# Half-array transposes, each half into its own PSUM bank, and all PSUM as one ring of four two-bank tiles

## The chip, the cores and the metric

The kernel runs on one core of a Trainium2 chip. The metric is the device time of one execution in microseconds. Engines are named as in the profile: PE (TensorE matmul), PEld (its weight loads), DVE (VectorE), ACT (ScalarE), POOL (GpSimd) and SP (SyncE, which issues the transfers).

## What is computed

Attention with a learned position bias, for 4 batches, 8 heads, 576 positions and head size 64, then a low-rank token mix and a channel MLP on the heads side by side (512 wide, hidden layer 2048):

```python
# attention: bias is a small MLP of the positions, for each head
scores = scale * np.matmul(q, k.transpose(0, 1, 3, 2))
h = np.maximum(x @ w1 + b1, 0.0)          # x[i, j] = log1p|i-j| / log1p(max(i, 1))
scores = scores + (h @ w2).transpose(2, 0, 1)[None]
attn = np.exp(scores - np.max(scores, axis=-1, keepdims=True))
attn = attn / (np.sum(attn, axis=-1, keepdims=True) + 1e-09)
o = np.matmul(attn, v)
# then, with x the heads side by side, (4, 576, 512)
u = x + (x.transpose(0, 2, 1) @ U @ V).transpose(0, 2, 1)
out = u + np.maximum(u @ w_ch1, 0.0) @ w_ch2
```

## The kernel before

The work goes in stages; the order on each engine is the order of the code (the schedule is manual).

**Bias** (0 to 68 us of the profiled execution). Tiles `bs` of the position MLP, written to DRAM and read back as `bias`. The first head pair is started among them.

**Attention** (68 to 396 us). Two heads are a pair; 16 pairs, each in nine slots, `slot(p, s)`. Slot 0 takes the last 64 rows of both heads, slots 1 to 8 one block of 128 query rows of one head. A slot's score product `sc` (L359) is made on PE by 64-row halves of the array: the two halves hold the same 64 numbers of head size against two halves of the keys, and write two banks of one tile. DVE adds the bias and takes the row minimum (L363), ACT takes the exponential (L382), and PE transposes the result, 128x128 blocks, by products with an identity: `tb` (L429, four blocks, in the slots 3 to 8 and in 0 and 1 of the pair behind), `tm` (L437), `ti` (L446, L449). DVE or ACT copies them to SBUF (L411 and L409 through `copy`). `av` (L465, tile `o`) multiplies with `v`: once for the first half of the query rows at the end of slot 8 (o0 from here on), once for the second half in slot 2 of the next pair (o1). `assemble` transposes its output back (`tx`, L483, L485). The slots carry other work besides: the conversion of the weights from 64-bit words (`conv_ops`: ACT L206, L209, DVE L212, L218, L224, POOL L229), the split of the next pair's operands into high and low parts on POOL (`hi` L178, `lo` L184), and from pair 4 on the token mix of the batch behind (`mt` L504, `mh` L523 to L525, in pairs 5, 9 and 13).

**MLP** (from 355 us, mixed with the end of attention until 396 us, alone after that). A round has two transposes of the input (`tu`, L581), `ph` (L608, 48 products), and `po` twice (L631, 24 products in all). `ph` is read by ACT (L613) and then DVE (L614), `po` by DVE (L634). In the rounds from 408 to 445 us DVE, ACT and POOL convert the next group's weights as well.

**PSUM** has eight banks. Before, `sc`, `bs` and `ph` come from two two-bank tiles (psS; a third, psX, while the bias stage lasts), `o` and every second `po` from one bank (psA), and all transposes, `mt`, `mh` and the other `po` from three single banks (psT and psT2).

The lines that decide which buffer a product waits for, and a transpose with its copy:

```python
rot = {"s": [psS], "t": [psT, psT2, psT2]}                   # after the bias stage
bank = psum("t", [P, 4, P], "tb")
for kb in range(4):
    nc.tensor.transpose(bank[:, kb, :], src[:, b0 + kb * P : b0 + (kb + 1) * P], ident)
copy(eng, pt[:, 5 * hd : 5 * hd + 4, o : o + P], bank)
```

Of the kernel before, what the change touches and what calls it, by code (L numbers as in the profile page):

```python
# [8 lines left out]
F32 = mybir.dt.float32  # L9
# [6 lines left out]
PSUM = bass.MemoryType.PSUM  # L16
# [4 lines left out]
DM = H * D  # L21
# [4 lines left out]
P = 128  # L26
# [25 lines left out]
def kernel(  # L52
# [282 lines left out]
    def scores(p, s):  # L335
# [4 lines left out]
        ps = psum("s", [P, 2, 512], "sc")  # L340
# [80 lines left out]

    def tr(p, c, hd, eng):
        hf, o = q_off(c)
        pt = get_pt(p, hf)
        src = pair[p]["P"][c]
        bank = psum("t", [P, 4, P], "tb")
        b0 = 0 if hd == 0 else S + LEFT
        for kb in range(4):
            nc.tensor.transpose(bank[:, kb, :], src[:, b0 + kb * P : b0 + (kb + 1) * P], ident)  # L429
        copy(eng, pt[:, 5 * hd : 5 * hd + 4, o : o + P], bank)  # L430

    def tr_m(p, eng):
        pt = get_pt(p, 0)
        pm = pair[p]["pm"]
        bank = psum("t", [P, 4, P], "tm")
        for kb in range(4):
            nc.tensor.transpose(bank[:, kb, :], pm[:, kb * P : (kb + 1) * P], ident)  # L437
        for hd in range(2):
            copy(eng, pt[:, 5 * hd : 5 * hd + 4, 0:LEFT], bank[:, :, hd * LEFT : (hd + 1) * LEFT])

    def tr_mid(p, hf, eng):
        pt = get_pt(p, hf)
        d = pair[p]
        bank = psum("t", [P, 4, P], "ti")
        for i in range(2):
            nc.tensor.transpose(bank[:, i, :], d["P"][2 * hf + i][:, 4 * P : 5 * P], ident)  # L446
        o = LEFT if hf == 0 else 0
        if hf == 0:
            nc.tensor.transpose(bank[:, 2, :], d["pm"][:, 4 * P : 5 * P], ident)  # L449
        copy(eng, pt[:, 4, o : o + 2 * P], bank[:, 0:2, :].rearrange("p a b -> p (a b)"))  # L450
        if hf == 0:
            copy(eng, pt[0:LEFT, 4, 0:LEFT], bank[0:LEFT, 2, 0:LEFT])
            copy(eng, pt[LEFT:P, 4, 0:LEFT], bank[LEFT:P, 2, LEFT:P])

    def av(p, hf):
        d = pair[p]
# [15 lines left out]
        ot = otp.tile([P, 320], F32, tag="ot", name="ot")
        copy("a", ot[:, 0:n], o[:, 0:n])
        d["ot", hf] = ot

    def assemble(p, hf):
# [3 lines left out]
        bank = psum("t", [P, 4, P], "tx")  # L480
        o = LEFT if hf == 0 else 0
        for i in range(2):
            nc.tensor.transpose(bank[:, i, :], ot[:, o + i * P : o + (i + 1) * P], ident)  # L483
        if hf == 0:
            nc.tensor.transpose(bank[0:LEFT, 2, :], ot[:, 0:LEFT], ident)  # L485
# [4 lines left out]
            in0=bank[:, 0:2, :].rearrange("p c (h d) -> p c h d", h=2),  # L490
# [3 lines left out]
        if hf == 0:  # L494
            copy("d", x_sb[0:LEFT, 4, hp * P : (hp + 1) * P], bank[0:LEFT, 2, :])
# [3 lines left out]
    def mix_t(b):  # L499
        t = psum("t", [P, DM], "mt")  # L500
# [77 lines left out]
    def make_ut(j, i):  # L578
        bank = psum("t", [P, KD, P], "tu")
# [16 lines left out]
    def mlp1(n):  # L596
# [23 lines left out]
    def mlp2(n):  # L620
# [3 lines left out]
        def step(i):  # L624
            ps = psA.tile([P, DM], F32, tag="a", name="po") if i % 2 else psum("t", [P, DM], "po")
# [340 lines left out]
```

## Time and profile before

| | us |
|---|---|
| median of 3 runs | 778.06 (776.85 to 778.28) |
| the profiled execution's own time | 778.02 |
| its span, first to last instruction | 776.0 |

| engine | busy us | share of the span |
|---|---|---|
| PE | 751.6 | 97% |
| DVE | 437.2 | 56% |
| ACT | 355.2 | 46% |
| POOL | 204.2 | 26% |

The share of busy time is a mean over stages with different limits, and a busy PE is not a PE at its peak: a matmul counts as busy while it is under way, and several are under way at once. Which wait ends last in a stage is read from timelines: one row is a run of like instructions on an engine, with its start, its duration, and in brackets the idle time ahead of it and what ended that.

### The profile page before, as it was taken

To read this page: it belongs to the slowest core of one execution; us is meant where nothing else is said; L and a number is where in the kernel's file an instruction comes from. 1 tells how busy PE (TensorE), PEld (TensorE's weight loads), DVE (VectorE), ACT (ScalarE), POOL (GpSimd) and SP (SyncE) were. 2 spreads that over 40 slices of the span, in tenths; PEclk is the share of its full clock that TensorE was granted. 3 is DMA by queue.
4 is the path that set the end of the run, shared out by engine and by line. 5 is a ranking of instruction groups with operands and counts; after the bars stand their busy time and mean duration, and the time that the engine had idled before them with its cause. 6 is when DMAs were issued, how large, how long until landed. Compare 5 with 4: busy or idle time off the path is not lost.

```text
span 776.0 us, 14159 instructions
## 1 busy us (share of the span) xinstructions
PE 751.6 (97%) x5452; PEld 593.7 (77%) x5452; DVE 437.2 (56%) x953; ACT 355.2 (46%) x827; POOL 204.2 (26%) x222
## 2 busy tenths in 40 slices
PE   6888999999999999999999999999999999999998
PEld 4325777666656675777889899889999999999886
DVE  7994577688877885663348844762147722221222
ACT  6995777677667775774115522441114410110010
POOL 0012545444444443630005601550005500000000
PEclk9999999999999999999999999999999999999999
DMA  5898953443344334540053300230003200001111
GB/s 182 277 312 267 292 158 93 134 133 107 106 140 133 109 94 116 160 166 2 21 191 97 109 13 28 89 102 1 1 14 96 69 1 1 1 28 55 55 41 68
DMA packets 46514, 78.77 MB, mean 102 GB/s; under 512 B 7920, under 2 KB 14576, under 8 KB 46448
## 3 DMA queue, kind: packets, MB, share of 16 engines
q1 hardware_dynamic: 46208, 77.62, 32.7%
q8 instruction: 43, 0.70, 0.4%
q10 hardware_dynamic: 240, 0.26, 0.1%
q14 instruction: 23, 0.19, 0.1%
HBM read 55.43 MB, written 22.43 MB: 100 GB/s over the span
## 4 chain that ended last, share of the span: by engine, by line
PE 78%; ACT 8%; DVE 8%; DMA 3%; issue 2%; POOL 1%; SPq 1%; ACTq 0%; DVEq 0%; POOLq 0%
PE po L631 24%; PE ph L608 23%; PE o L465 8%; PE sc L359 8%; PE tb L429 6%; PE bs L287 3%; DVE wt L218 2%; ACT p L382 2%; ACT pt L409 1%; DVE p L363 1%; PE tm L437 1%; PE mt L504 1%; DVE wt L212 1%; PE tx L483 1%; ACT ring L275 1%
## 5 line engine op out<-in xcount | busy, mean ns | idle before, releaser
L613 ACT ACTIVATE hh<-ph 128x1024 fp32r<-128x1024 f32 x36 | 36.9, 1026 | 207.2 <-PE ph L608 207.2
L614 DVE SCALAR_TENSOR_TENSOR hh<-ph,hh 128x1024 fp32r<-128x1024 f32 x36 | 44.1, 1225 | 140.2 <-ACT hh L613 140.2
L229 POOL TENSOR_TENSOR wy<-wt,wy 128x256 int32<-128x256 int32 (+1 forms) x68 | 50.0, 735 | 272.9 <-DVE wt L224 244.7
L382 ACT ACTIVATE p<-p,st 128x576 f32<-128x576 f32 x128 | 99.9, 781 | 38.1 <-DVE st L363 38.1
L363 DVE CUSTOM_DVE_ANT_0 p<-sc,bias 128x576 f32<-128x576 f32 x128 | 96.2, 751 | 25.8 <-PE sc L359 16.8
L631 PE MATMUL po<-wq,hh 128*128 128x512 f32 x432 | 103.2, 394 | 0.0
L631 PE MATMUL po<-w2q,hh 128*128 128x512 f32 x432 | 101.7, 390 | 0.4 <-DVE acc L634 0.4
L608 PE MATMUL ph<-ut,w1q 128*128 128x256 f32 x768 | 94.0, 280 | 0.0
L608 PEld LDWEIGHTS ph<-ut,w1q 128*128 128x128 f32 x768 | 91.9, 188 | 2.1 <-issue 1.2
L631 PEld LDWEIGHTS po<-wq,hh 128*128 128x128 f32 x432 | 80.1, 188 | 17.5
L631 PEld LDWEIGHTS po<-w2q,hh 128*128 128x128 f32 x432 | 79.9, 188 | 16.7 <-issue 0.6
L608 PEld LDWEIGHTS ph<-ut,wq 128*128 128x128 f32 x768 | 90.0, 188 | 1.4
L634 DVE TENSOR_TENSOR acc<-po,acc 128x512 f32<-128x512 f32 x72 | 49.6, 689 | 73.1 <-PE po L631 73.1
L608 PE MATMUL ph<-ut,wq 128*128 128x256 f32 x768 | 90.2, 277 | 0.0
L465 PE MATMUL o<-pt,v 128*64 128x320 f32 (+1 forms) x640 | 88.7, 411 | 0.6 <-ACT pt L409 0.6
L429 PE MATMUL tb<-ident,p 128*128 128x128 f32 x512 | 82.2, 283 | 3.4 <-DVE x_sb L411 1.8
L465 PEld LDWEIGHTS o<-pt,v 128*64 128x64 f32 x640 | 50.8, 136 | 27.6 <-issue 3.0
L429 PEld LDWEIGHTS tb<-ident,p 128*128 128x128 f32 x512 | 55.0, 140 | 20.9 <-issue 11.7
L409 ACT COPY pt<-tb 128x512 f32<-128x512 f32 x88 | 50.9, 579 | 30.4 <-PE tb L429 30.2
L359 PE MATMUL sc<-hi 64*128 64x288 f32 (+1 forms) x320 | 62.4, 386 | 1.9 <-DVE st L363 1.8
L184 POOL TENSOR_TENSOR lo<-raw,hi 128x896 fp32r<-128x896 f32 x30 | 63.2, 2108 | 2.2
L359 PEld LDWEIGHTS sc<-hi 64*128 64x128 f32 (+1 forms) x320 | 29.0, 178 | 40.0 <-issue 32.1
(94 smaller groups left out, 1024.6 us busy)
## 6 DMA issues: line engine op xcount, KB each, us to landing
wraw<-in_w_ch_dram SPq DMA_DIRECT2D x64, 256.0 KB, 2.7
raw<-in_qk_dram SPq DMA_DIRECT2D x32, 288.0 KB, 4.6
bias_dram<-ring SPq DMA_DIRECT2D x26, 295.5 KB, 3.3
v<-in_vp_dram SPq DMA_DIRECT2D x16, 320.0 KB, 3.6
bias<-bias_dram SPq DMA_DIRECT2D x16, 288.0 KB, 4.4
acc<-u_dram SPq DMA_DIRECT2D x18, 256.0 KB, 4.9
out_dram<-acc SPq DMA_DIRECT2D x18, 256.0 KB, 2.0
bias<-bias_dram SPq DMA_DIRECT2D x16, 256.0 KB, 4.9
```

The source lines that it names most:

```text
L184: eng.tensor_tensor(out=lo[:, a:e], in0=raw[:, a:e], in1=hi[:, a:e].bitcast(F32), op=ALU.subtract)
L229: nc.gpsimd.tensor_tensor(out=st["y"], in0=st["t"], in1=st["y"], op=ALU.add)
L359: mm(ps[0:n, a, 0:HALF], lhsT=q[r, q0 : q0 + n], rhs=k[r, k0 : k0 + HALF], start=(i == 0), stop=(i == len(terms) - 1),)
L363: nc.vector.tensor_tensor_reduce(out=halves(dst), in0=ps[:, :, 0:HALF], in1=halves(bias[hp][:, s * S : (s + 1) * S]), scale=-0.125, scalar ...
L382: nc.scalar.activation(out=dst, in_=dst, func=AF.Exp, bias=st[:, s : s + 1], scale=-1.0, accum_out=st[:, 10 + s : 11 + s])
L409: nc.scalar.copy(out=out, in_=in_)
L429: nc.tensor.transpose(bank[:, kb, :], src[:, b0 + kb * P : b0 + (kb + 1) * P], ident)
L465: mm(o[hd * D : (hd + 1) * D, 0:n], lhsT=v[:, vb * D : (vb + 1) * D], rhs=pt[:, pb, :], start=(j == 0), stop=(j == 4),)
L608: mm(st["ps"][:, f, :], lhsT=w, rhs=u[:, k, :], start=(i == 0), stop=(i == 3 * KD - 1))
L614: nc.vector.scalar_tensor_tensor(out=hl[n], in0=st["ps"], scalar=0.0, in1=hh[n].bitcast(F32), op0=ALU.max, op1=ALU.subtract)
L631: mm(ps, lhsT=h, rhs=w, start=(m == 0), stop=(m == 3 * FG - 1))
L634: nc.vector.tensor_tensor(out=a, in0=ps, in1=a, op=ALU.add)
```

## The change

Every transpose of attention is made by two products of half the rows. The source's rows 0 to 63 go through the upper half of the array into one bank, rows 64 to 127 through the lower half into the next bank. The copies read both banks at once and put the halves side by side; they move as many elements as before. The transposes `tu` of the MLP stay whole. And PSUM becomes one ring: each tile of the program, whatever it holds, takes two banks, and the buffer of the fourth tile before it.

```diff
-    psS = ctx.enter_context(tc.tile_pool(name="psS", bufs=2, space=PSUM))
-    psT = ctx.enter_context(tc.tile_pool(name="psT", bufs=1, space=PSUM))
-    psA = ctx.enter_context(tc.tile_pool(name="psA", bufs=1, space=PSUM))
...
-    def psum(tag, shape, name):
-        rot[tag].append(rot[tag].pop(0))
-        return rot[tag][-1].tile(shape, F32, tag=tag, name=name)
+    ps4 = ctx.enter_context(tc.tile_pool(name="ps4", bufs=4, space=PSUM))
+
+    def psum(name):
+        return ps4.tile([P, 2, 512], F32, tag="ps", name=name)
...
+    def flip(bank, i, src, a):
+
+        for h in range(2):
+            r = slice(h * D, (h + 1) * D)
+            nc.tensor.transpose(bank[:, h, i * D : (i + 1) * D], src[r, a : a + P], ident[r, r])
+
     def tr(p, c, hd, eng):
...
-        bank = psum("t", [P, 4, P], "tb")
+        bank = psum("tb")
         b0 = 0 if hd == 0 else S + LEFT
         for kb in range(4):
-            nc.tensor.transpose(bank[:, kb, :], src[:, b0 + kb * P : b0 + (kb + 1) * P], ident)
-        copy(eng, pt[:, 5 * hd : 5 * hd + 4, o : o + P], bank)
+            flip(bank, kb, pair[p]["P"][c], b0 + kb * P)
+        copy(
+            eng,
+            pt[:, 5 * hd : 5 * hd + 4, o : o + P].rearrange("p k (h q) -> p h k q", h=2),
+            bank[:, :, 0 : 4 * D].rearrange("p h (k q) -> p h k q", k=4),
+        )
...
-        o = psA.tile([P, 512], F32, tag="a", name="o")
+        o = psum("o")[:, 0, :]
...
-        bank = psum("t", [P, KD, P], "tu")
+        bank = psum("tu")[:, 0, :].rearrange("p (k q) -> p k q", k=KD)
...
-                st["ps"] = psum("s", [P, FG, TB], "ph")
+                st["ps"] = psum("ph").rearrange("p a (b t) -> p (a b) t", t=TB)
...
-            ps = psA.tile([P, DM], F32, tag="a", name="po") if i % 2 else psum("t", [P, DM], "po")
+            ps = psum("po")[:, 0, :]
```

`tm`, `ti` and `tx` are changed as `tb` is, `mt`, `mh`, `sc` and `bs` take their tile as `o` and `ph` do.

On PE, the end of a pair: slot 8's scores, the transposes of the last attention output (`tx`) and of slot 8 (`tb`), and the first product of o0. Before:

```order
L359 MATMUL sc<-hi 128x288 [waits DVE_49]
L359 MATMUL sc<-hi 128x288
L359 MATMUL sc<-lo,hi 128x288 x2
L359 MATMUL sc<-hi,lo 128x288 x2
L483 MATMUL tx<-ident,ot 128x128 [waits Activation_49]
L483 MATMUL tx<-ident,ot 128x128
L429 MATMUL tb<-ident,p 128x128 [waits DVE_49,PE_49,Activation_49]
L429 MATMUL tb<-ident,p 128x128 x3
L465 MATMUL o<-pt,v 64x320 [waits DMAHW7_49]
```

The same place after:

```order
L352 MATMUL sc<-hi 128x288 [waits Activation_49]
L352 MATMUL sc<-hi 128x288
L352 MATMUL sc<-lo,hi 128x288 x2
L352 MATMUL sc<-hi,lo 128x288 x2
L419 MATMUL tx<-ident,ot 128x64 [waits DVE_49,PE_49]
L419 MATMUL tx<-ident,ot 128x64 x3
L419 MATMUL tb<-ident,p 128x64 [waits DVE_49,Activation_49]
L419 MATMUL tb<-ident,p 128x64 x7
L471 MATMUL o<-pt,v 64x320 [waits DMAHW7_49,DVE_49]
```

Six whole transposes have become twelve halves, and o0, which waited for no other engine's work on PSUM, waits for DVE now: the fourth tile before it is the `tb` of slot 7, which DVE copies out. In pair 0 it is the score tile of slot 7.

On PE, one round of the MLP while weights are converted (`ut` is the transposed input, `w1q` and `w2q` the weights, `hh` the hidden layer). Before:

```order
L581 MATMUL tu<-ident,acc 128x128 [waits DMAHW1_49,DVE_49]
L581 MATMUL tu<-ident,acc 128x128 x3
L581 MATMUL tu<-ident,acc 128x128 [waits DMAHW2_49,DVE_49]
L581 MATMUL tu<-ident,acc 128x128 x3
L608 MATMUL ph<-ut,w1q 128x256 [waits Activation_49]
L608 MATMUL ph<-ut,w1q 128x256 x47
L631 MATMUL po<-w2q,hh 128x512 [waits DVE_49,Activation_49]
L631 MATMUL po<-w2q,hh 128x512 x11
```

After:

```order
L591 MATMUL tu<-ident,acc 128x128 [waits DMAHW5_49,DVE_49]
L591 MATMUL tu<-ident,acc 128x128 x3
L591 MATMUL tu<-ident,acc 128x128 [waits DMAHW6_49,DVE_49]
L591 MATMUL tu<-ident,acc 128x128 x3
L618 MATMUL ph<-ut,w1q 128x256 [waits DVE_49,Activation_49]
L618 MATMUL ph<-ut,w1q 128x256 x47
L641 MATMUL po<-w2q,hh 128x512 [waits DVE_49,Activation_49]
L641 MATMUL po<-w2q,hh 128x512 x11
```

The products are the same. `ph` waits for DVE besides: a round has five tiles, so the fourth tile before `ph` is the first `po` of the round behind, which DVE adds to the accumulator (L634). The second `tu` takes the buffer of the `ph` of the round behind.

## Rows read from the trace of the kernel before

**Rows 1.** Page, part 4: the chain that ended last, share of the span by engine and line

```profile
PE po L631 24%; PE ph L608 23%; PE o L465 8%; PE sc L359 8%; PE tb L429 6%; PE bs L287 3%; DVE wt L218 2%; ACT p L382 2%; ACT pt L409 1%; DVE p L363 1%; PE tm L437 1%; PE mt L504 1%; DVE wt L212 1%; PE tx L483 1%; ACT ring L275 1%
```

**Rows 2.** Busy us of each engine in a stretch, granted clock, DMA share, GB/s

```profile
core 0: us, PE busy (x) PEld busy (x) DVE busy (x) ACT busy (x) POOL busy (x), PEclk, DMA share, GB/s
42.20:45.50 3.30, 3.23 (x24) 0.81 (x24) 3.30 (x11) 3.30 (x9) 0.00 (x0) 0.50 0.94 302
80.00:356.00 276.00, 271.01 (x2194) 186.69 (x2193) 198.47 (x508) 194.51 (x486) 122.79 (x114) 1.00 0.47 135
```

**Rows 3.** Timeline of PE, pair 7: start, duration, engine, line, operation, count, idle before

```profile
181.22 0.29 PE L359 MATMUL sc<-lo,hi 64*64 64x288 f32 x2
181.36 0.29 PE L359 MATMUL sc<-hi,lo 64*64 64x288 f32 x2
...
182.76 0.66 PE L429 MATMUL tb<-ident,p 128*128 128x128 f32 x4
183.25 0.38 PE L446 MATMUL ti<-ident,p 128*128 128x128 f32 x2
...
195.89 2.91 PE L465 MATMUL o<-pt,v 128*64 128x320 f32 x20
```

**Rows 4.** Timeline of PEld, pair 7, slots 1 and 2

```profile
182.16 0.19 PEld L359 LDWEIGHTS sc<-hi 64*128 64x128 f32 x2 [0.17 <-issue]
...
182.76 0.42 PEld L429 LDWEIGHTS tb<-ident,p 128*128 128x128 f32 x4 [0.17 <-issue]
```

**Rows 5.** Timeline of DVE, pair 7

```profile
185.56 0.88 DVE L212 TENSOR_SCALAR wt<-wt 128x256 f32<-128x256 f32 x1 [0.52 <-ACT wt L206]
186.47 2.15 DVE L218 TENSOR_SCALAR wt<-wt 128x256 int32<-128x256 int32 x1
188.55 0.74 DVE L363 CUSTOM_DVE_ANT_0 p<-sc,bias 128x576 f32<-128x576 f32 x1
...
195.44 0.69 DVE L411 COPY pt<-tb 128x512 f32<-128x512 f32 x1
...
199.94 0.76 DVE L363 CUSTOM_DVE_ANT_0 praw<-sc,bias 128x576 f32<-128x576 f32 x1 [2.29 <-PE sc L359]
```

**Rows 6.** Timeline of ACT, pair 7

```profile
191.91 0.65 ACT L409 COPY pt<-tm 128x256 f32<-128x256 f32 x2 [0.44 <-PE tm L437]
```

**Rows 7.** Timeline of POOL, pair 7

```profile
185.35 0.94 POOL L178 TENSOR_SCALAR hi<-raw 128x896 fp32r<-128x896 f32 x1
186.38 2.10 POOL L184 TENSOR_TENSOR lo<-raw,hi 128x896 fp32r<-128x896 f32 x1
```

**Rows 8.** Timeline of DVE, pair 3

```profile
110.56 0.29 DVE L218 TENSOR_SCALAR wt<-wt 128x256 int32<-128x256 int32 x1
111.56 0.76 DVE L363 CUSTOM_DVE_ANT_0 p<-sc,bias 128x576 f32<-128x576 f32 x1 [0.71 <-PE sc L359]
...
115.86 0.76 DVE L363 CUSTOM_DVE_ANT_0 p<-sc,bias 128x576 f32<-128x576 f32 x1 [0.25 <-PE sc L359]
```

**Rows 9.** Timeline of DVE, end of pair 0

```profile
68.02 0.76 DVE L363 CUSTOM_DVE_ANT_0 p<-sc,bias 128x576 f32<-128x576 f32 x1 [4.98 <-DMA bias<-bias_dram]
```

**Rows 10.** Timeline of PE, end of pair 0, start of pair 1

```profile
64.22 2.91 PE L465 MATMUL o<-pt,v 128*64 128x320 f32 x20
68.93 0.40 PE L359 MATMUL sc<-hi 64*128 64x288 f32 x2 [1.80 <-DVE st L363]
```

**Rows 11.** Timeline of PE, MLP rounds with weight conversion

```profile
409.04 5.69 PE L608 MATMUL ph<-ut,w1q 128*128 128x256 f32 x48
...
432.62 5.69 PE L608 MATMUL ph<-ut,w1q 128*128 128x256 f32 x48
438.75 5.71 PE L631 MATMUL po<-w2q,hh 128*128 128x512 f32 x24 [0.45 <-DVE acc L634]
```

**Rows 12.** Timeline of DVE, MLP rounds with weight conversion

```profile
410.45 0.68 DVE L634 TENSOR_TENSOR acc<-po,acc 128x512 f32<-128x512 f32 x1
...
437.92 0.69 DVE L634 TENSOR_TENSOR acc<-po,acc 128x512 f32<-128x512 f32 x1
```

More of the change, by code (lines that the diff above doesn't have):

```diff
@@ L76 @@
     dram = ctx.enter_context(tc.tile_pool(name="dram", bufs=1, space=DRAM))
-    psS = ctx.enter_context(tc.tile_pool(name="psS", bufs=2, space=PSUM))
-    psT = ctx.enter_context(tc.tile_pool(name="psT", bufs=1, space=PSUM))
-    psA = ctx.enter_context(tc.tile_pool(name="psA", bufs=1, space=PSUM))
-    p0 = ExitStack()
-    psX = p0.enter_context(tc.tile_pool(name="psX", bufs=1, space=PSUM))
-    rot = {"s": [psS, psS, psX], "t": [psT]}
-    def psum(tag, shape, name):
-        rot[tag].append(rot[tag].pop(0))
-        return rot[tag][-1].tile(shape, F32, tag=tag, name=name)
+    ps4 = ctx.enter_context(tc.tile_pool(name="ps4", bufs=4, space=PSUM))
+    def psum(name):
+        return ps4.tile([P, 2, 512], F32, tag="ps", name=name)
     big = ctx.enter_context(tc.tile_pool(name="big", bufs=1, side="right"))
@@ L283, in bias_mm @@
         n = reach(T)[2]
-        bs[T] = psum("s", [P, 2, 512], "bs")
+        bs[T] = psum("bs")
         for a in range(0, n, 512):
@@ L339, in scores @@
         st = d["st"]
-        ps = psum("s", [P, 2, 512], "sc")
+        ps = psum("sc")
         if s == 0:
@@ L424, in tr @@
         pt = get_pt(p, hf)
-        src = pair[p]["P"][c]
-        bank = psum("t", [P, 4, P], "tb")
+        bank = psum("tb")
         b0 = 0 if hd == 0 else S + LEFT
         for kb in range(4):
-            nc.tensor.transpose(bank[:, kb, :], src[:, b0 + kb * P : b0 + (kb + 1) * P], ident)
-        copy(eng, pt[:, 5 * hd : 5 * hd + 4, o : o + P], bank)
+            flip(bank, kb, pair[p]["P"][c], b0 + kb * P)
[4 more added lines that the diff above has]
+        )
     def tr_m(p, eng):
         pt = get_pt(p, 0)
-        pm = pair[p]["pm"]
-        bank = psum("t", [P, 4, P], "tm")
+        bank = psum("tm")
         for kb in range(4):
-            nc.tensor.transpose(bank[:, kb, :], pm[:, kb * P : (kb + 1) * P], ident)
+            flip(bank, kb, pair[p]["pm"], kb * P)
         for hd in range(2):
-            copy(eng, pt[:, 5 * hd : 5 * hd + 4, 0:LEFT], bank[:, :, hd * LEFT : (hd + 1) * LEFT])
+            copy(eng, pt[:, 5 * hd : 5 * hd + 4, 0:LEFT], bank[:, hd, 0 : 4 * D].rearrange("p (k q) -> p k q", k=4))
     def tr_mid(p, hf, eng):
@@ L443, in tr_mid @@
         d = pair[p]
-        bank = psum("t", [P, 4, P], "ti")
+        bank = psum("ti")
         for i in range(2):
-            nc.tensor.transpose(bank[:, i, :], d["P"][2 * hf + i][:, 4 * P : 5 * P], ident)
+            flip(bank, i, d["P"][2 * hf + i], 4 * P)
         o = LEFT if hf == 0 else 0
         if hf == 0:
-            nc.tensor.transpose(bank[:, 2, :], d["pm"][:, 4 * P : 5 * P], ident)
-        copy(eng, pt[:, 4, o : o + 2 * P], bank[:, 0:2, :].rearrange("p a b -> p (a b)"))
+            flip(bank, 2, d["pm"], 4 * P)
+        copy(
+            eng,
+            pt[:, 4, o : o + 2 * P].rearrange("p (i h q) -> p h i q", i=2, h=2),
+            bank[:, :, 0 : 2 * D].rearrange("p h (i q) -> p h i q", i=2),
+        )
         if hf == 0:
-            copy(eng, pt[0:LEFT, 4, 0:LEFT], bank[0:LEFT, 2, 0:LEFT])
-            copy(eng, pt[LEFT:P, 4, 0:LEFT], bank[LEFT:P, 2, LEFT:P])
+            for h in range(2):
+                r = slice(h * LEFT, (h + 1) * LEFT)
+                copy(eng, pt[r, 4, 0:LEFT], bank[r, h, 2 * D : 3 * D])
     def av(p, hf):
@@ L479, in assemble @@
         hp = p % HP
-        bank = psum("t", [P, 4, P], "tx")
+        bank = psum("tx")
         o = LEFT if hf == 0 else 0
         for i in range(2):
-            nc.tensor.transpose(bank[:, i, :], ot[:, o + i * P : o + (i + 1) * P], ident)
+            flip(bank, i, ot, o + i * P)
         if hf == 0:
-            nc.tensor.transpose(bank[0:LEFT, 2, :], ot[:, 0:LEFT], ident)
+            flip(bank, 2, ot, 0)
         xs = x_sb[:, 2 * hf : 2 * hf + 2, hp * P : (hp + 1) * P].rearrange("p c (h d) -> p c h d", h=2)
@@ L489, in assemble @@
             out=xs,
-            in0=bank[:, 0:2, :].rearrange("p c (h d) -> p c h d", h=2),
+            in0=bank[:, :, 0 : 2 * D].rearrange("p h (c d) -> p c h d", c=2),
             in1=r.unsqueeze(3).to_broadcast([P, 2, 2, D]),
@@ L494, in assemble @@
         if hf == 0:
-            copy("d", x_sb[0:LEFT, 4, hp * P : (hp + 1) * P], bank[0:LEFT, 2, :])
+            copy(
+                "d",
+                x_sb[0:LEFT, 4, hp * P : (hp + 1) * P].rearrange("p (h d) -> p h d", h=2),
+                bank[0:LEFT, :, 2 * D : 3 * D],
+            )
     mixt = {}
     def mix_t(b):
-        t = psum("t", [P, DM], "mt")
+        t = psum("mt")[:, 0, :]
         for c in range(5):
@@ L520, in mix_h @@
         n = P if c < 4 else LEFT
-        h = psum("t", [P, DM], "mh")
+        h = psum("mh")[:, 0, :]
         vh, vl = v4h[:, c * P : (c + 1) * P], v4l[:, c * P : (c + 1) * P]
@@ L728 @@
             slot(0, early[i])
-    p0.close()
-    psT2 = ctx.enter_context(tc.tile_pool(name="psT2", bufs=2, space=PSUM))
-    rot = {"s": [psS], "t": [psT, psT2, psT2]}
     loads[0:0] = bias_loads(3, 0)
```

## The prediction

> **What bounds the kernel now.** I read the chain of waits first, then the stretches, then the timelines stage by stage. The chain runs for 47% of the span through `po` and `ph` of the MLP and for some 25% through PE work of attention (`o`, `sc`, `tb`, `tm`, `tx`); DVE and ACT lines stand between them with 1 to 2% each [rows 1]. In attention PE counts as busy for 271.0 of 276.0 us, DVE for 198.5 and ACT for 194.5 [rows 2]. The reader should not take the 271 for a wall: the timelines of a pair show three parts with different limits.
>
> First part, from a pair's first reduction to that of slot 3. In pair 7, DVE's shift (L218) stands for 2.15 us and the clamp ahead of it for 0.88 [rows 5], while POOL makes `hi` (0.94) and `lo` (2.10) [rows 7]; the shift and `lo` end at about the same time, and slot 3's reduction follows at once, at 188.55. In pair 3 the same shift takes 0.29, and slot 3 waits 0.71 us for PE [rows 8]. So in pairs like 7 (6, 7, 8, 10, 11, 12, and in their way the mix pairs 5, 9, 13) this part is a matter of DVE against POOL, in pairs like 3 (2, 3, 14, with the mix ahead of slot 0 also 4) it hangs on PE in a small part.
>
> Second part, from slot 3 to o0 (188.55 to 195.89 in pair 7). DVE does one reduction and one copy a slot nearly without a gap; the last copy starts at 195.44 and ends at 196.13, after o0 has begun [rows 5, 3]. Of these 7.34 us DVE is idle for about 0.4. In pair 3 one such gap is 0.25, put down to PE [rows 8]; the three gaps of that pair add to 0.66.
>
> Third part, o0 to the next pair's first reduction, 195.89 to 199.94: 2.91 of `o` and the score product of slot 0; DVE waits 2.29 for it [rows 3, 5]. Nothing in it is a transpose.
>
> **The change part by part.** *Transposes by halves.* Four whole ones take 0.49 us until the next transpose begins (182.76 to 183.25), 0.12 each. The nearest row for a half one is the score product that already runs by 64 rows: a pair of halves issues every 0.14 with 288 columns moving [rows 3]. A half transpose moves 64. The cost of two halves thus lies between 0.06 (the halves run together, each with half the columns) and 0.14 (they cost what a score pair costs); I take 0.06 to 0.07, because the weights are the larger part and their load of 0.42 for four [rows 4] is split over both halves. Besides, PE changes between score form and transpose form twice a slot, and the weight loads stand still for 0.17 at each change [rows 4]; scores and half transposes have one form, so these go. For a pair that is 46 x 0.05 = 2.3 plus some 14 x 0.17 = 2.4, so PE needs 4.7 us less of a pair's 17.4 to 18.2. Little of it lies on the path, as the three parts show.
>
> *The copies.* They have pieces of 64 where they had 128. ACT's `tm` copies, two of 256 in pieces of 64, take 0.65 together [rows 6]; one of 512 in pieces of 128 takes 0.69 on DVE [rows 5]. So I cost it at nothing; the upper bound is 0.1 for a copy.
>
> *The ring in attention.* o0 now takes the buffer of slot 7's `tb` and waits for DVE's copy of it, to 196.13 instead of 195.89: +0.24 in every pair [rows 5, 3]. The Trainium skill, TensorEngine Tiling (Array Packing), "Gotcha 1: PSUM Pressure", says that row tiling raises the demand on PSUM because each row tile needs a bank of its own; this wait is what it comes to here. The same page, "PSUM Bottleneck", has the copies out of PSUM as the next limit once TensorE is faster; by that rule alone the second part would be worth only DVE's gaps, which is how I count it.
>
> The pairs then come to: 2, 3, 14: gaps 0.66 and about 0.25 ahead of slot 3, less 0.24, so -0.66 each, and 4 likewise; 14, whose last gaps are longer, some 0.5 more; together -3.2. Pairs 7, 8, 10, 11: 0.4 of gaps and a little of the start, less 0.24, -0.23 each, -0.9. Pairs 6 and 12 have no such gaps: +0.23 each, +0.5. The mix pairs 5, 9, 13, where the chain passes through more PE work, -0.5 to -1.1, together -2.2. Pair 15 -0.3. **Sum -6.2**, with bounds -12 (all gaps and the POOL stalls' entry go) and +3.8 (16 x 0.24, nothing gained).
>
> *The ring at the start.* In pair 0, DVE waits 4.98 for the bias transfer and reduces slot 7 at 68.02 [rows 9]. o0 ran in that time, at 64.22; PE then waited for slot 7 with the next scores until 68.93 [rows 10]. After the change o0's buffer is the score tile of slot 7, so o0 waits for 68.02 + 0.76 = 68.78, and the next scores come at 68.8 + 2.9 = 71.7, 2.8 late. Pair 1 makes most of this good, since PE needs 4.7 less there: +0.1 is left (bounds 0 and 2.8). But PE has then been idle for 4.9 us. After the one long idle time in the trace the granted clock was 0.50, the 1.2 GHz level, for 3.3 us [rows 2]; that would cost up to 1.65 of PE work, and I put 1.3. **+1.4.**
>
> *The tail of attention (355 to 396).* `ph` is a form of its own, so the half transposes between its steps now need changes that whole ones did not: 7 x 0.17, less 15 x 0.05. **+0.5.**
>
> *The ring in the MLP.* A round is `tu`, `tu`, `ph`, `po`, `po`: five tiles on four buffers. `ph` waits until DVE has added the first `po` of the round behind, the second `tu` until DVE has made the low part of the last `ph`. While weights are converted, DVE is late, held by its own queue behind ACT and POOL, and not by PE. The additions: 410.45 + 0.68 = 411.13 and in the third round 437.92 + 0.69 = 438.61 [rows 12]; `ph` began at 409.04 and 432.62 [rows 11]. So `ph` of the first of these rounds starts 2.1 late, of the second 4.4, of the third 6.0, and these are one growing delay, not three to be added. Of it the 0.45 that `po` waited at 438.75 [rows 11] goes. **+5.6.** Behind these instructions nothing is released late on DVE that PE would need, and later rounds have no conversion ahead of the additions, so it is neither made good nor enlarged. Lower bound 0 (if the conversion chain moves ahead against PE), upper bound 8.
>
> Sum against the profiled execution's own 778.02: 1.4 - 6.2 + 0.5 + 5.6 = +1.3, so **779.3**. The three runs' median is 778.06, the same.
>
> **The rivals.** *A, faster: DVE wins against POOL in the pairs like 7.* The clamp begins at 185.56, 0.2 after POOL's `hi` at 185.35 [rows 5, 7]. If earlier transposes move ACT's part ahead by more than that, clamp and shift run in 0.6 before POOL and slot 3 comes at least 1.1 earlier, in six pairs: -6.6, 772.7. For it: ACT's queue ahead of the clamp holds two copies of `tb`. Against it: I find only 0.15 of movement there.
>
> *B, slower: the halves run one after the other, or the banks hold them apart, so that a pair of halves costs 0.12 to 0.14.* The change then doesn't do what it says. The forms' changes are still saved, so the pairs stand at about zero: 778.0 + 1.4 + 0.5 + 5.6 = 785.5. It decides from 0.12 for two halves. Against it: the score halves issue a pair every 0.14 with 288 columns [rows 3].
>
> *C, slower: the clock falls in the MLP too.* Each of the three waits ahead of `ph` (2.1, 2.3 and 1.6 us) leaves PE idle. If each is followed by 3.3 us at 1.2 GHz as in [rows 2], each costs up to 1.65: +5, 784.3. Against it: PE waited 1.80 ahead of 68.93, and the product there took its usual 0.40 [rows 10].
>
> *D, faster: the MLP wait is made good*, because DVE's late additions turn out to be late only behind PE. Then +5.6 falls to about 1: 774.7.
>
> **How the numbers follow.** The measurement can tell 0.2%, 1.6 us, from no change: 776.5 to 779.6. The forecast, with its own spread of about 3 us either way, has 0.60: of it 0.08 falls faster, 0.29 same, 0.23 slower. A has 0.10 and D 0.06, both faster; B 0.12 and C 0.10 slower; 0.02 is left and goes to same. Together faster 0.24, same 0.31, slower 0.45. The forecast's own range is 776 to 782; with the rivals the range is 773.0 to 785.5.
>
> **What would show it.** In the trace after: half transposes at 0.06 to 0.07 for two and no gap between scores and `tb`; o0 named as waiting for DVE, in pair 0 until 68.8 with a granted clock below 1 behind it; slot 3 of pairs like 7 still right behind the shift; `ph` in the rounds from 400 us on waiting for DVE's addition, about 6 us in all. The prediction is wrong if the attention stage ends more than 9 or less than 2 us earlier, or if the MLP's waits come to less than 3 us.

## The result and the profile after

The changed kernel takes 783.45 us (median of 5 runs, 783.12 to 786.80) where the kernel before takes 777.80 in the same comparison: 1.0083 times as long, with a 95% interval of 1.0061 to 1.0105. It is slower. The forecast was 779.3 with a range of 773.0 to 785.5; the range holds the time, the likeliest value is 4 us short. One execution of the kernel of experiment 6, of 3494 us, is left out of its median.

The page of the changed kernel, busy time by engine and the chain of waits:

```profile
PE 723.1 (93%) x6188; PEld 574.1 (73%) x6188; DVE 432.7 (55%) x953; ACT 356.4 (46%) x827; POOL 203.8 (26%) x222
...
PE 63%; DVE 17%; ACT 8%; DMA 4%; issue 4%; POOL 2%; SPq 1%; DVEq 0%; ACTq 0%; POOLq 0%
PE ph L618 24%; PE po L641 23%; PE o L471 8%; DVE p L356 4%; ACT p L375 3%; DVE pt L404 2%; PE sc L352 2%; DVE wt L211 2%; DVE ring L270 2%; PE bs L280 2%; DVE wt L217 2%; ACT pt L402 1%; DVE wt L205 1%; PE mt L514 1%; DMA u_dram<-x_sb 1%
```

PE's busy time has fallen by 28.5 us and the span has grown by 5.3. In the chain, PE stands with 63% where it had 78%, and DVE with 17% where it had 8%: the reduction (L356) and the copies (L404) of attention have taken the place that the transposes had in [rows 1].

Where the 5.3 us came from, by the start of like instructions in the two traces (the profiled execution of the changed kernel is the fastest of its five):

| stretch | later than before at its end | added in the stretch | forecast |
|---|---|---|---|
| start, to pair 2's first reduction (88.45 before, 89.11 after) | +0.66 | +0.7 | +1.4 |
| pairs 2 to 15, to the last o0 (352.22, 351.49) | -0.73 | -1.4 | -6.2 |
| tail, to the MLP's first round with conversion (408.25, 408.02) | -0.23 | +0.5 | +0.5 |
| MLP with conversion, to the `ph` behind it (445.09, 450.35) | +5.26 | +5.5 | +5.6 |

Three of the four terms came out within 0.7 us. One is off by 4.8: the pairs. The start's is partly luck: in the kernels of the experiments 2 and 3, which have the same code up to there, pair 2's first reduction came at 91.02 and 90.73, 2.6 and 2.3 later than before.

**The halves do what they say.** PE in pair 7, slot 1 and slot 8 (start, duration, operation, count, idle before):

```profile
182.19 0.41 PE L419 MATMUL tb<-ident,p 64*128 64x64 f32 x8
182.41 0.38 PE L352 MATMUL sc<-hi 64*128 64x288 f32 x2
...
195.88 0.46 PE L419 MATMUL tb<-ident,p 64*128 64x64 f32 x8 [0.98 <-DVE st L356]
196.39 2.91 PE L471 MATMUL o<-pt,v 128*64 128x320 f32 x20
```

The eight halves of a `tb` and the change to the next scores take 0.22 (182.19 to 182.41), 0.055 for two halves, without a stop between. Against the 0.12 of a whole transpose [rows 3] that is less than half the time. The last two rows show what became of it: `tb` of slot 8 waits 0.98 for DVE's reduction of slot 7, whose buffer it takes, and o0 starts at 196.39. DVE in the same pair:

```profile
187.13 2.15 DVE L211 TENSOR_SCALAR wt<-wt 128x256 int32<-128x256 int32 x1
189.21 0.74 DVE L356 CUSTOM_DVE_ANT_0 p<-sc,bias 128x576 f32<-128x576 f32 x1
...
195.65 0.69 DVE L404 COPY pt<-tb 128x512 f32<-128x512 f32 x1
```

The shift still takes 2.15 and slot 3 still follows it, as in [rows 5]; the copy of slot 7's `tb` begins at 195.65 and o0 follows its end. The pair takes 17.94 where it took 18.15: 0.21 less, forecast 0.23.

**The MLP.** PE in the rounds with conversion, the rows that answer to [rows 11]:

```profile
410.05 0.66 PE L591 MATMUL tu<-ident,acc 128*128 128x128 f32 x4 [1.43 <-DVE hh L624]
411.13 7.40 PE L618 MATMUL ph<-ut,w1q 128*128 128x256 f32 x48 [0.43 <-DVE acc L644]
...
425.21 5.89 PE L618 MATMUL ph<-ut,w1q 128*128 128x256 f32 x48 [0.34 <-DVE acc L644]
...
438.57 5.68 PE L618 MATMUL ph<-ut,w1q 128*128 128x256 f32 x48 [1.08 <-DVE acc L644]
...
450.35 5.69 PE L618 MATMUL ph<-ut,w1q 128*128 128x256 f32 x48
```

The second `tu` waits for DVE's low part of the last `ph`, each `ph` for DVE's addition: the waits of the forecast, at the places of the forecast. The first `ph` takes 7.40 and not 5.69, at half clock, but the next one waits for DVE anyway, so this costs nothing: the three rounds follow each other by 14.10 and 13.36 us, and in experiment 1, where the clock stays at 1.00 there, by 14.09 and 13.37.

**The start.** PE at the end of pair 0, the rows that answer to [rows 10]:

```profile
62.12 0.46 PE L419 MATMUL tb<-ident,p 64*128 64x64 f32 x8 [0.24 <-ACT p L375]
67.67 4.43 PE L471 MATMUL o<-pt,v 128*64 128x320 f32 x20 [5.09 <-DVE st L356]
72.03 0.40 PE L352 MATMUL sc<-hi 64*128 64x288 f32 x2
```

o0 waits 5.09 for DVE's reduction of slot 7 and then takes 4.4 instead of 2.9. This is the clock: stretches with a granted clock below 1 in the changed kernel (busy us of PE, PEld, DVE, ACT, POOL; then the clock, the DMA share, GB/s):

```profile
64.00:72.00 8.00, 4.33 (x20) 1.90 (x20) 2.04 (x5) 2.44 (x6) 1.77 (x1) 0.58 0.89 261
132.00:140.00 8.00, 6.49 (x58) 3.77 (x58) 5.07 (x14) 4.68 (x13) 2.55 (x2) 0.79 0.55 137
172.00:180.00 8.00, 7.17 (x92) 5.95 (x90) 7.58 (x22) 6.62 (x18) 2.67 (x2) 0.79 0.20 48
268.00:276.00 8.00, 7.27 (x88) 5.98 (x90) 7.19 (x21) 6.59 (x18) 2.27 (x2) 0.79 0.54 128
412.00:416.00 4.00, 4.00 (x23) 4.00 (x22) 3.42 (x7) 2.34 (x6) 2.25 (x4) 0.57 0.32 105
```

The kernel before has none between 75 and 390 us. Here the clock falls to 0.50, the 1.2 GHz level, for 6.8 us at the start (64 to 71), where PE is idle for 5.09, but also for 3.4 us each at 136, 173 and 269 us, where no single idle time ahead of the fall was longer than 1.5.

### The profile page after: what moved, and what is told of

Same layout as the page of the kernel before. It is cut to its first block, busy times and chain, and to the rows that moved or that the text cites. A ratio compares the mean times of both kernels' runs of the same rounds, so it can differ in the third digit from the quotient of the medians.

```text
span 781.3 us, 15654 instructions
## 1 busy us (share of the span) xinstructions
PE 723.1 (93%) x6188; PEld 574.1 (73%) x6188; DVE 432.7 (55%) x953; ACT 356.4 (46%) x827; POOL 203.8 (26%) x222
## 4 chain that ended last, share of the span: by engine, by line
PE 63%; DVE 17%; ACT 8%; DMA 4%; issue 4%; POOL 2%; SPq 1%; DVEq 0%; ACTq 0%; POOLq 0%
PE ph L618 24%; PE po L641 23%; PE o L471 8%; DVE p L356 4%; ACT p L375 3%; DVE pt L404 2%; PE sc L352 2%; DVE wt L211 2%; DVE ring L270 2%; PE bs L280 2%; DVE wt L217 2%; ACT pt L402 1%; DVE wt L205 1%; PE mt L514 1%; DMA u_dram<-x_sb 1%
## 5 line engine op out<-in xcount | busy, mean ns | idle before, releaser
L356 DVE CUSTOM_DVE_ANT_0 p<-sc,bias 128x576 f32<-128x576 f32 x128 | 95.3, 745 | 21.2 <-PE sc L352 14.8
L471 PE MATMUL o<-pt,v 128*64 128x320 f32 (+1 forms) x640 | 94.9, 423 | 10.4 <-DVE st L356 7.8
L618 PE MATMUL ph<-ut,w1q 128*128 128x256 f32 x768 | 96.1, 283 | 2.2 <-DVE acc L644 1.9
L618 PEld LDWEIGHTS ph<-ut,w1q 128*128 128x128 f32 x768 | 93.8, 191 | 5.4 <-issue 3.7
L471 PEld LDWEIGHTS o<-pt,v 128*64 128x64 f32 x640 | 46.4, 140 | 48.0 <-DVE st L356 10.6
L419 PE MATMUL tb<-ident,p 64*128 64x64 f32 x1024 | 57.1, 230 | 20.1 <-DVE st L356 17.1
L419 PEld LDWEIGHTS tb<-ident,p 64*128 64x128 f32 x1024 | 48.6, 141 | 31.0 <-issue 13.1
L280 PE MATMUL bs<-ring,small_sb 128*32 128x512 f32 (+17 forms) x352 | 42.5, 512 | 11.4 <-ACT ring L268 10.9
```

The source lines that it names most:

```text
L280: mm(bs[T][32 * cg : 32 * cg + 32, a // 512, 0 : min(n - a, 512)], lhsT=w2_sb, rhs=hids[T][cg][:, a : min(n, a + 512)], start=True, stop=True,
L356: nc.vector.tensor_tensor_reduce(out=halves(dst), in0=ps[:, :, 0:HALF], in1=halves(bias[hp][:, s * S : (s + 1) * S]), scale=-0.125, scalar ...
L419: nc.tensor.transpose(bank[:, h, i * D : (i + 1) * D], src[r, a : a + P], ident[r, r])
L471: mm(o[hd * D : (hd + 1) * D, 0:n], lhsT=v[:, vb * D : (vb + 1) * D], rhs=pt[:, pb, :], start=(j == 0), stop=(j == 4),)
L618: mm(st["ps"][:, f, :], lhsT=w, rhs=u[:, k, :], start=(i == 0), stop=(i == 3 * KD - 1))
```

## The experiments

**1. The ring alone.** Every transpose whole again and into one bank of its two-bank tile, which the copies then read; all else as changed:

```diff
     def flip(bank, i, src, a):
-        for h in range(2):
-            r = slice(h * D, (h + 1) * D)
-            nc.tensor.transpose(bank[:, h, i * D : (i + 1) * D], src[r, a : a + P], ident[r, r])
+        n = src.shape[0]
+        nc.tensor.transpose(bank[:, 0, i * P : i * P + n], src[:, a : a + P], ident[0:n, 0:n])
...
```

> The ring of four two-bank tiles as in the changed kernel, but every transpose whole and into one bank, as before. It leaves the halves out, so it shows the ring alone. Theory: the MLP's waits are those of the changed kernel (5.5 us), the start loses 2.8 us and pair 1 has nothing to make it good with, each pair's o0 waits about 0.2 longer for DVE's copy (3 us): 778 + 11 = 789 us, and the granted clock stays near 1 in pairs 2 to 15 because PE has as much to do as before. Rival (the halves gain nothing, and the ring alone makes the loss): 783.5 us, the same as the changed kernel.

Measured: 790.30 us, 1.0159 times the kernel before (1.0137 to 1.0181). The ring alone costs 12.5 us, and the halves give back 6.9. Pair 7 of this kernel on PE:

```profile
199.41 0.63 PE L418 MATMUL tb<-ident,p 128*128 128x128 f32 x4
199.97 2.91 PE L462 MATMUL o<-pt,v 128*64 128x320 f32 x20
```

o0 comes at 199.97, when DVE's copy of slot 7's `tb` is done; slot 3 to o0 takes 7.60 where it took 7.34 before, so the wait of 0.24 is there at 0.26, and at 0.25 to 0.26 in the pairs 8, 10 and 11. It is not the same in every pair: the pairs 2 and 14 take as long as before (7.68 and 7.71 against 7.68), 6 and 12 take 0.65 more. Its MLP waits are those of the changed kernel:

```profile
417.09 5.89 PE L609 MATMUL ph<-ut,w1q 128*128 128x256 f32 x48 [0.43 <-DVE acc L635]
...
431.18 5.89 PE L609 MATMUL ph<-ut,w1q 128*128 128x256 f32 x48 [1.11 <-DVE acc L635]
...
444.55 5.68 PE L609 MATMUL ph<-ut,w1q 128*128 128x256 f32 x48 [1.08 <-DVE acc L635]
```

And the clock between 75 and 390 us, here and then in the changed kernel:

```profile
75.00:390.00 315.00, 309.09 (x2459) 214.99 (x2459) 211.55 (x534) 206.44 (x507) 126.87 (x118) 1.00 0.42 121
```

```profile
75.00:390.00 315.00, 281.40 (x3184) 200.27 (x3183) 210.81 (x534) 208.07 (x507) 126.72 (x118) 0.98 0.43 123
```

With whole transposes PE is busy for 309 us of this stretch and the clock stays at 1.00; with halves it is busy for 281, and the clock's mean is 0.98.

**2. Two halves of a round in one tile of the ring.** In the MLP the two `tu` share a two-bank tile, and so do the two `po`. `half` takes a new tile for the first of two and its second bank for the other:

```diff
-            ps = psum("po")[:, 0, :]
+            ps = half("po", n, i, n >= 2)
...
```

> In the MLP after the end of attention the two transposes of a round share one two-bank tile of the ring, and the two po share another; nothing else differs from the changed kernel. A round then has three tiles on four buffers instead of five. Theory 1 (the ring makes ph wait for DVE's addition of the round behind, 5.3 to 5.5 us in all): the waits ahead of ph at 411, 425 and 438 us go, and the dip of the clock behind the first of them; 783.45 - 5.3 = 778.1 us. Rival (DVE, ACT and POOL were late only because PE was late, so that another product waits for them instead): less than 2 us of it comes back, 782 us.

Measured: 834.73 us, 1.0731 times the kernel before. The edit brought a wait of its own, of 1.3 to 3.2 us twice a round while weights are converted (PE, the second `po` and the second `tu` of a round), and of 0.8 to 1.3 ahead of the second `po` in the rounds after that:

```profile
411.65 4.50 PE L650 MATMUL po<-w2q,hh 128*128 128x512 f32 x12 [3.16 <-DVE acc L653]
...
418.14 0.66 PE L600 MATMUL tu<-ident,acc 128*128 128x128 f32 x4 [1.55 <-DVE ut L603]
```

The second half's first product waits until DVE has read the first half: the two halves of one tile are ordered as a whole, though they are different banks. So this run tells nothing of theory 1. Its attention is instruction for instruction that of the changed kernel, and its stretches at half clock lie elsewhere (between 208 and 216, 248 and 256, and 312 and 316 us). This is used below. The same edit together with the one of experiment 4:

> Both of the above at once. If theories 1 and 2 hold and are independent, the two gains add: 783.45 - 5.3 - 2.9 = 775.2 us, faster than the kernel before. If only the first holds, 778 us; if only the second, 780.5 us.

gave 844.84 us, 1.0862 times the kernel before. It has the same wait, and settles nothing about theory 1 either.

**3. Pools of their own for the MLP.** The ring is closed at the end of attention; `ph` then has two two-bank tiles, `tu` and `po` have four single banks:

```diff
     p1.close()
+    pr.close()
+    late["s"] = ctx.enter_context(tc.tile_pool(name="psS", bufs=2, space=PSUM))
+    late["t"] = ctx.enter_context(tc.tile_pool(name="psT", bufs=4, space=PSUM))
...
```

> After attention the ring is closed, and the MLP takes two two-bank tiles for ph and four single banks for tu and po; attention is that of the changed kernel. Theory 1 (the ring makes ph wait for DVE's addition of the round behind): the 5.3 to 5.5 us of the stretch from 408 to 445 us come back whole, 783.4 - 5.4 = 778.0 us. Rival (DVE's lateness would have held another product there): less than 2 us back, 782 us.

Measured: 777.71 us, 1.0008 times the kernel before (0.9993 to 1.0023): 5.7 us less than the changed kernel. PE in the rounds with conversion:

```profile
412.82 5.69 PE L624 MATMUL ph<-ut,w1q 128*128 128x256 f32 x48
...
424.60 5.69 PE L624 MATMUL ph<-ut,w1q 128*128 128x256 f32 x48
...
436.39 5.69 PE L624 MATMUL ph<-ut,w1q 128*128 128x256 f32 x48
...
448.18 3.99 PE L624 MATMUL ph<-ut,w1q 128*128 128x256 f32 x33
```

Each round follows the last by 11.79 us, with no wait; even the 0.45 of [rows 11] is gone. (The first round comes late, at 412.82, because attention ended later in this execution; pair 13 alone took 23.44 us there and 21.78 in the changed kernel.) Theory 1 stands: the ring made PE wait for DVE, and DVE's lateness holds nothing else up.

**4. Every half transpose twice.**

```diff
-            nc.tensor.transpose(bank[:, h, i * D : (i + 1) * D], src[r, a : a + P], ident[r, r])
+            for _ in range(2):
+                nc.tensor.transpose(bank[:, h, i * D : (i + 1) * D], src[r, a : a + P], ident[r, r])
```

> Every half transpose is issued twice, with the same result; nothing else differs from the changed kernel. PE has some 2.5 us more to do in a pair, and is still not what the pairs wait for. Theory 2 (what is missing of the gain in attention went to stretches at half clock, at 135 to 139, 173 to 176 and 268 to 271 us, which come when PE has been idle): the granted clock stays at 1.00 in attention after the start, pairs 4, 6 and 11 lose about 2.9 us, 780.5 us. Rival (the clock costs nothing there, the pairs are held by DVE's copies and reductions): no dips either way count, 783.5 to 785 us, and the doubled transposes push some slots later.

Theory 2 is that the missing gain of attention went to the stretches at half clock. Measured: 796.04 us, 1.0226 times the kernel before (1.0205 to 1.0246), above both values that were expected (780.5, and 783.5 to 785). The clock stayed at 1 from 76 to 360 us, as theory 2 expected, but pairs like 7 took 18.43 us instead of 17.94. The end of pair 7, on PE:

```profile
202.15 0.72 PE L420 MATMUL tb<-ident,p 64*128 64x64 f32 x16 [0.65 <-DVE st L356]
202.79 0.49 PE L472 MATMUL o<-pt,v 128*64 128x320 f32 x2
```

`tb` of slot 8 may begin only when DVE has reduced slot 7; o0 starts when this `tb`, now 0.64 long, is done. So a transpose that stands behind such a wait is on the path with its whole length: the expectation's sentence that PE is not what the pairs wait for was wrong there, and the run prices the clock only in mixture with this.

**5. Repeats only in front of the waits.** The halves of `tx`, which stand ahead of the waiting `tb` in slots 4 and 8, six times each:

```diff
-            flip(bank, i, ot, o + i * P)
+            flip(bank, i, ot, o + i * P, 6)
...
```

> The half transposes of tx, which stand ahead of the two places of a pair where PE waits longest for DVE (slots 4 and 8), are issued six times each, with the same result, so that PE is idle for less there: some 0.8 and 0.55 us of work go into waits of 1.1 and 1.0. All else as in the changed kernel. Theory 2 (stretches at half clock cost attention some 2.5 us, and come where PE has been idle): no such stretch between 75 and 390 us, and the pairs keep 17.9 us where they lost the most, 781 us. Rival (the clock falls as often, or the repeats cost what it gave): 783.4 us or more.

Measured: 793.08 us, 1.0207 times the kernel before (1.0183 to 1.0231). The pairs 6, 7, 10 and 11 came out at 17.93 to 17.94, 8 and 12 at 20.02 to 20.03, with the clock at 1.00: what theory 2 expected of them. It had expected no fall at all between 75 and 390 us, though, and there were three, at 158 and 239 (in the mix pairs 5 and 9) and at 359 us. The mix pairs 5 and 9 took 3 us more, and 1, 14 and 15 about 1 each, so the time is the rival's. DVE in pair 9:

```profile
237.46 0.42 DVE L495 TENSOR_TENSOR x_sb<-tx,st 128x256 f32<-128x256 f32 x1 [3.46 <-DMA u_dram<-x_sb]
```

It waits 3.46 us for a store of `x_sb`, which landed 4.0 after its issue, not 2.0 as in the changed kernel. Why it landed later was not tried. In this mix pair the store is what sets slot 5, and not PE.

**6. Pair 0's transposes ahead of slot 7's scores.**

```diff
         new, old = p < NP, p > 0
+        if p == 0 and s == 7:
+            tr(p, 2, 0, "d")
+            tr(p, 2, 1, "a")
         if new:
             scores(p, s)
...
```

> In pair 0 alone, the transposes of the slots 7 and 8 come ahead of the scores of slot 7, so that o0 of this pair takes a buffer which does not wait for the reduction held by the bias transfer. All else as in the changed kernel. Theory 3 (o0's wait at the start and the half clock behind it cost pair 1 some 3 us that it does not make good whole): pair 1's first reduction comes about 3 us earlier, at 70 us, and the granted clock does not fall there; pair 2 starts 2 to 3 us earlier, 780.5 to 781.5 us. Rival (pair 1 makes it good anyway, so nothing of it is left): 783 us.

Measured: 780.58 us, 1.0036 times the kernel before (1.0020 to 1.0052): 2.9 less than the changed kernel. PE at the same place as above:

```profile
65.18 4.34 PE L471 MATMUL o<-pt,v 128*64 128x320 f32 x20
69.45 0.40 PE L352 MATMUL sc<-hi 64*128 64x288 f32 x2
```

o0 no longer waits for the bias transfer, and the next scores come at 69.45 instead of 72.03. Pair 1's first reduction comes at 70.55, 2.6 earlier, and pair 2's at 87.48, 1.6 earlier. The clock was expected not to fall, and it did, at 64.7: o0 is still at half clock, and the idle times of PE ahead of it were 0.5, 0.5 and 1.57.

**7. The edits together.** First all three (pools, pair 0, `tx` six times everywhere):

> The three edits above at once: pools of their own for the MLP, pair 0's transposes ahead of slot 7's scores, tx issued six times. If the three gains are independent: 783.4 - 5.4 - 2.5 - 2.5 = 773.0 us, faster than the kernel before. If the clock's part is nothing: 775.5 us; if only the MLP's waits are real, 778 us.

Measured: 783.37 us, 1.0077 times the kernel before (1.0060 to 1.0094); the repeats cost what the two others gave, most of it in the mix pairs 5 and 9 (24.05 and 23.87, in the changed kernel 20.70 and 21.37). Then the two that stood, without repeats:

> Two edits of the runs before at once: pools of their own for the MLP, and pair 0's transposes ahead of slot 7's scores. If what the changed kernel lost lay in these two places and the places are independent: 777.7 - 2.4 = 775.3 us, faster than the kernel before by 0.3%. If pair 0's gain is lost again in attention's end: 777.7 us.

Measured: 775.93 us, 0.9974 times the kernel before (0.9960 to 0.9988). The two gains add to within about 1 us: 783.45 - 5.7 - 2.9 = 774.8. And with the repeats only in the six pairs where they had cost nothing:

```diff
-            flip(bank, i, ot, o + i * P)
+            flip(bank, i, ot, o + i * P, 6 if p + 1 in (6, 7, 8, 10, 11, 12) else 1)
...
```

> As the run with both edits, and tx issued six times in the pairs 6, 7, 8, 10, 11 and 12 alone, where the repeats cost nothing in the run that had them everywhere (17.94 us a pair, 20.02 with the mix). Theory 2 for these pairs (a stretch at half clock there costs 0.1 to 0.4 us): no stretch between 165 and 300 us, 0.5 us less, 774.8 us. Rival (a stretch only moves into other pairs): 775.3 us or more.

Measured: 773.64 us, 0.9937 times the kernel before (0.9920 to 0.9954), the fastest of all. The stretch from 165 to 300 us without and with the repeats:

```profile
165.00:300.00 135.00, 116.77 (x1394) 81.47 (x1392) 106.11 (x260) 95.24 (x238) 60.12 (x57) 0.97 0.41 113
```

```profile
165.00:300.00 135.00, 127.87 (x1693) 91.33 (x1691) 104.68 (x256) 94.02 (x234) 61.04 (x57) 1.00 0.41 110
```

With useless work of 11 us on PE the granted clock of this stretch is 1.00 and not 0.97. The kernel became 2.3 us faster, and the intervals of the two against the kernel before do not meet. But the 2.3 us are not the price of the clock in these pairs. From pair 6's first reduction to pair 13's the two profiled executions take 133.39 and 133.17 us: 0.22 less, where theory 2 expected 0.5. They differ most in the pairs 1, 4 and 13, whose code is the same (19.39, 21.06 and 23.71 us without the repeats, 17.16, 19.36 and 20.56 with them); why those came out shorter is open.

**8. The same two edits with whole transposes.**

> The ring in attention with whole transposes (the halves are left out), the MLP with pools of its own, pair 0's transposes ahead of slot 7's scores: the halves' worth where the ring's two places are mended. From the run of the ring with whole transposes the halves are worth 790.3 - 783.4 = 6.9 us, so 775.9 + 6.9 = 782.8 us, and the granted clock stays near 1. Rival (the halves' worth is mostly that they make good the wait at the start, which is mended here): 778 us, the kernel before.

Measured: 783.02 us, 1.0064 times the kernel before (1.0047 to 1.0081). The halves are worth 783.0 - 775.9 = 7.1 us, nearly the 6.9 of the first experiment, with the start and the MLP mended as without. The rival (778 us) fell.

## Why the prediction was right and wrong

The time lies in the range, and the ring's price in the MLP was right. But the prediction was to be wrong if attention ended less than 2 us earlier, and that happened: the last o0 came 0.73 earlier, the MLP's first round with conversion 0.23. (Its sum for the pairs adds to -6.1, not -6.2; nothing hangs on the difference.)

**The halves' price: right.** 0.055 for two halves, forecast 0.06 to 0.07; the changes of form went. Rival B (one half after the other) fell.

**The ring in the MLP: right**, +5.5 for +5.6, shown by experiment 3. The steps of the sum, 2.1, then 4.4, then 6.0 as one growing delay, are the rows at 411.13, 425.21 and 438.57. Rival D fell.

**The start: right in its mechanism**, o0 waiting for slot 7's reduction and half clock behind it; DVE's reduction behind the transfer came 1.17 us earlier than in the trace of before (66.85, 68.02), which made the term smaller. Experiment 6 takes o0's wait away.

**o0's wait: right in pairs like 7**, 0.26 for 0.24 (experiment 1), but not "in every pair": with whole transposes it is nothing in 2 and 14 and 0.65 in 6 and 12. The page named in the prediction (the Trainium skill, TensorEngine Tiling (Array Packing), "Gotcha 1: PSUM Pressure") says that row tiles need banks of their own; no run here put both halves into one bank. What the runs show is the price of the ring that provides the banks, 12.5 us against the 6.9 that the halves gave, and that 5.7 us come back when the MLP has pools of its own. Its "PSUM Bottleneck" says that copies out of PSUM can become the limit; the trace agrees in pair 7, where o0 (196.39) now follows DVE's copy (195.65 + 0.69).

**The pairs: wrong, the term that was mis-sized.** It was put at -6.2 and came to -1.4. The 4.8 us are in four places, of which the first is the largest (pair 2 gained 0.5 more than forecast, pair 14 0.3 less):

- *The clock, about 2.5.* The prediction let the clock fall at the start, and in rival C in the MLP, but nowhere in attention, where PE is idle only for short times. It took the fall in [rows 2] for one behind "the one long idle time in the trace". That reading was wrong: the idle times of PE ahead of that fall (at 42.16) were short as well, two pieces with 0.75 of work between them. PE in the kernel before:

```profile
40.18 0.75 PE L287 MATMUL bs<-ring,small_sb 128*32 128x320 f32 x8 [1.78 <-ACT ring L302]
42.27 4.00 PE L287 MATMUL bs<-ring,small_sb 128*32 128x336 f32 x28 [1.34 <-DVE st L363]
```

  In the changed kernel it fell in the pairs 4, 6 and 11. The price is read from kernels with the same attention code whose stretches lie elsewhere. Pair 4's o0 and the mix behind it, in the changed kernel and then in the kernel of experiment 3:

```profile
135.70 4.54 PE L471 MATMUL o<-pt,v 128*64 128x320 f32 x20
140.18 2.04 PE L514 MATMUL mt<-x_sb,u_sb 128*32 128x512 f32 x10
```

```profile
137.31 2.91 PE L477 MATMUL o<-pt,v 128*64 128x320 f32 x20
140.15 2.04 PE L520 MATMUL mt<-x_sb,u_sb 128*32 128x512 f32 x10
```

The 20 products take 4.5 at half clock and 2.9 at full: 1.6. Pair 6 took 18.33 against 17.93, pair 11 18.36 against 17.93: 0.4 each. The clock of the same stretches in the kernel of experiment 3, whose low stretches in attention lie at 210, 250, 312 and 353 us:

```profile
132.00:140.00 8.00, 6.43 (x88) 4.38 (x86) 6.68 (x19) 6.31 (x17) 4.07 (x4) 1.00 0.35 95
208.00:216.00 8.00, 7.62 (x90) 6.19 (x92) 7.30 (x22) 6.92 (x19) 2.47 (x2) 0.79 0.29 79
248.00:256.00 8.00, 6.20 (x84) 5.55 (x86) 7.69 (x21) 5.68 (x15) 3.88 (x4) 0.79 0.08 18
```

So the places differ between runs of the same attention code, and the price differs with the place: 0.1 to 0.4 in the pairs 6 to 12, 1.6 in pair 4. That the falls come with PE's idle times is borne out by counting them in the pairs 6, 7, 8, 10, 11 and 12 of all profiled executions: two in each of the five kernels with halves and no repeats, none in the five with repeats (experiments 4, 5 and 7, and the combined run of experiment 2), none in the three with whole transposes. In the twelve executions of experiment 3 the time goes with the clock: 780.3 to 780.9 us in the four at 0.980 to 0.985, 775.6 to 779.8 in the eight at 0.987 to 0.991; but whatever makes PE wait lengthens the run and lowers the clock at once, so this is no price. The Trainium skill, TensorE: Matmul & The Clock Gate, "A second HAM failure mode: psum-queue depth-cycling", describes a kernel whose PE paused often and shortly between groups of products while it went round the PSUM banks, and whose clock went up and down for that; the trace agrees in part: PE was idle for 1.46 ahead of 135.19 and the clock was 0.50 behind it, but in experiment 3 it was idle for 1.44 at the same place (136.79) and the clock stayed at 1.00. The same page, "Part 4: PE-mode transpose", has transposes not count as PE work for the clock in the way that products do; here repeats of transposes alone took the falls away in six pairs (1.00 for 0.97), so here they do count. Whether they count as much as products was not measured.
- *The mix pairs, 1.2.* The forecast took 0.5 to 1.1 from each. Pair 5 gave 0.55, pair 9 0.17 (with the 0.35 of the next item in it), and pair 13 lost 0.06. Pair 13 was held by the store of `x_sb`. DVE there

```profile
310.23 0.42 DVE L494 TENSOR_TENSOR x_sb<-tx,st 128x256 f32<-128x256 f32 x1 [3.07 <-DMA u_dram<-x_sb]
```

  waited 3.07 for it. Before, the same row waited 1.64 for the same store (at 308.97), a wait that the prediction did not look for. The store landed 2.2 after its issue before, 3.6 here, and 3.9 to 4.3 in the four other kernels with halves and no repeats, whose pair 13 took 22.5 to 23.7 us. Where it landed in 2.4 (the last kernel of experiment 7), pair 13 took 20.56, 1.2 less than before, which is what the forecast wanted. Why the store lands late was not tried.
- *Pairs 3 and 9, 0.35 each.* The next pair's first reduction starts 4.40 behind o0 where it was 4.06. The ring with whole transposes has it too (4.40 in both), so it is not the halves; the row names the `tb` behind the scores:

```profile
122.50 0.76 DVE L356 CUSTOM_DVE_ANT_0 praw<-sc,bias 128x576 f32<-128x576 f32 x1 [2.92 <-PE tb L419]
```

  What releases it was not settled.
- *Pair 4, 0.5.* DVE's join of the weight conversion took 0.97 there and 0.35 before, beside POOL:

```profile
133.28 0.97 DVE L217 SCALAR_TENSOR_TENSOR wt<-wraw,sgn,wt 128x128 int32<-128x128 int32 x1
```

**The rivals.** A (DVE wins against POOL) did not happen: the shift still takes 2.15. C was right in that the clock falls where PE waits in the MLP, wrong in the price: one `ph` took 1.7 longer, and the next wait for DVE swallowed it.

**The sign.** The sum ended at +1.3 because two large terms of opposite sign nearly cancelled, and the attention term was the less certain one; 0.45 was given to slower, the largest of the three chances. That the range holds the time owes something to luck: the pairs' gain was missed, and the start's term came out small in this execution.

## What to carry to other kernels

One ring for all tiles ties each product to the reader of the fourth tile before it; count the tiles of each stage's round against the buffers, and give a stage whose readers are late for other reasons (here DVE in the weight conversion) buffers of its own. When PE is made faster than its neighbours, look up what its granted clock does: the idle time that was won can cost the clock. Look in the trace of before at what PE did ahead of each fall, every idle time and not only the longest. And after a step is taken from PE, ask stage by stage which wait is next; in three kinds of pairs it was three different ones (a copy, POOL against DVE, a store). A stretch whose clock rose is not yet the place where the time came from; compare the two traces there, pair by pair.

## What the runs showed of the hardware

Two half transposes, 64 rows each into a bank of its own, take 0.055 us together, where a whole one takes 0.12. In the changed kernel the granted clock fell to 0.50 three times in attention, for 3.4 us each, with no single idle time of PE above 1.5 us ahead of the fall; PE was busy for 281 of 315 us there, and the places differed between runs of the same attention code. With whole transposes (busy for 309 of 315 us) it did not fall. Repeated half transposes kept it at 1.00 in the six pairs where they filled part of PE's idle times. A store of 256 KB in a mix pair landed 2.0 us after its issue in one kernel and 4.0 at the same place in another (pair 9, the changed kernel and experiment 5).
